# All twelve gate and val chunks by seven products, the stores of narrowed blocks moved to SyncE, small products kept in front of two y columns only

## The chip, the cores and the metric

The kernel runs on one core of a Trainium2 chip. The metric is the time on the device in microseconds (us), the median over several runs. The engines are TensorE (PE; its weight loads are shown as PEld), VectorE (DVE), ScalarE (ACT), GpSimd (POOL) and SyncE (SP), which here only issues transfers.

## What is computed

The reference is an attention layer followed by two feed-forward layers, on 896 tokens (2 batches of 448) with 12 heads of 64:

```python
attn = softmax(mask(q @ k.T / 8)); x = (attn @ v)           # 896 x 768
h = x @ w_in                                                # 768 -> 2048
g = where(h >= 1, h, where(h <= -1, 0, (h + 1) ** 2 / 4))
y = g @ w_out                                               # 2048 -> 768
out = (silu(y @ w_gate) * (y @ w_val)) @ w_out2             # 768 -> 1536 -> 768
```

The weights reach the kernel as 64 bit floats, and the kernel itself makes 32 bit floats of them.

## The kernel before

**Number form.** A value is held as a high part and a low part, both in the reduced form fp32r: ScalarE casts the high part, VectorE subtracts it from the value for the low part (`split`). A product of two such values is three matmuls: high by high, high by low, low by high. All matmuls of the later stages have 128 x 128 weights and 448 columns.

**Stages.** The tokens are two groups g of 448 columns. First come attention and, mixed into it, the first half of h = x w_in (in 16 chunks f of 128 rows). Then follow the rest of h, and y = g w_out in 6 columns d of 128 rows, each cut in three (`OUT_CUTS`) with both groups in turn. Then come gate and val, in 12 chunks f, and last the product with w_out2 (the last stage), in seven products k with three pairs p each.

**Eight and seven products.** A chunk of gate and val is a product of a 2 x 2 block matrix (gate and val by the two halves of y's rows) with a 2 x 2 block matrix (halves by groups). `eight(f, ws)` does it directly: 8 block products of 9 matmuls. `seven(f, ws)` uses Strassen's scheme in Winograd's form: 7 block products of 9 matmuls, for which sums of weight blocks and of blocks of y are needed. T1 to T4 are the sums of y; they are collected in `sums12` and `sums34` while y is made (L735 to L739), finished with the last column (L756 to L758) and split into the tiles `th` and `tl` (T[0] to T[3]). `SEVEN` lists the chunks by seven: 1 to 10. Chunks 0 and 11 go by eight. In `seven`, products 1 and 2 use gate weights and Y of group 0, product 3 sums of weights and T[1], product 4 T[0], product 5 T[2], product 6 Y of group 1 (second half) and product 7 T[3]. Products 1, 3, 5 and 7 add up in the same PSUM tile, which ScalarE copies out to `one`, `two` and `three` after products 1, 3 and 5. The sums of weights (`Weights.sums`) are `ws`, with the parts `sh`, `sl`, `vh`, `vl`.

**Weights.** The class `Weights` prepares the weights in the order of their use: load (SP), narrow from 64 to 32 bits (`narrow`, three VectorE operations, L110, L113, L116), cast and subtract (L221, L222). Four buffers hold the parts; `room` says whether the next may be started, and `tick` issues a step of this work after a product. So the order written in the program follows the products; a scheduler then sets the order on each engine.

**Narrowed aside.** `narrow_apart` narrows the chunks in `APART` (3, 4, 6, 8, 9) and the blocks W21 of w_out2 during y, in 26 half blocks of 128 x 384 (`araw` into `at`), and stores them in HBM, from where they come back as 32 bit floats. SP loads the raw blocks into two buffers, ACT issues the stores. `S_TICKS` is the number of its steps issued after each third of a column and group (one more in the first third).

**Small products.** `strip` is a matmul of one weight column and eight columns of data whose result nobody reads. It stands in front of chunks 1 and 2 of h (`STRIPS`), of y columns 0 and 3 (`Y_STRIPS`, for both groups), of gate and val chunks 1 and 5 (`V_STRIPS`) and of the first product of the last stage.

**Last stage.** `u_terms` makes the terms of u for the seven products, each from u of chunks 0 to 5 (Z11, Z12) or 6 to 11 (Z21, Z22). W11 and W12 are narrowed into tiles of the pool `quads`; W21 and W22 come from HBM.

Of the kernel before, what the change touches and what calls it, by code (L numbers as in the profile page):

```python
# [8 lines left out]
F32 = mybir.dt.float32  # L9
# [14 lines left out]
N = 448  # L24
# [4 lines left out]
WB = 768  # L29
# [17 lines left out]
SEVEN = (1, 2, 3, 4, 5, 6, 7, 8, 9, 10)  # L47
TICK8 = (1, 2)
PIN0, PIN1 = 2, 28
APART = (3, 4, 6, 8, 9)  # L50
# [4 lines left out]
S_TICKS = 2  # L55
S_LOW = "V"
PINNED = 2
STRIPS = (1, 2)
Y_STRIPS = (0, 3)
V_STRIPS = (1, 5)  # L60
# [13 lines left out]
def fused_kernel(ctx: ExitStack, tc: tile.TileContext, qk, v, w_in, w_out, w_gv, w_o2, out):  # L74
# [47 lines left out]
    def narrow_apart(pool):  # L122

        parts = [(narrowed, f, w_gv[f], k) for f in APART for k in range(0, 2 * WB, PART)]
        parts += [(stored, ("W21", p), w_o2[p, 1, 0], k) for p in range(OUT_PAIRS) for k in range(0, WB, PART)]
# [11 lines left out]
        for p, (home, f, src, k) in enumerate(parts):  # L137
# [9 lines left out]
            if p:  # L147
                nc.scalar.dma_start(out=outs[p - 1][0], in_=outs[p - 1][1])
        nc.scalar.dma_start(out=outs[-1][0], in_=outs[-1][1])

    class Weights:
# [24 lines left out]
        def room(self, i):  # L176

            if I_GV <= i < I_O2 and (i - I_GV) % 2 and (i - I_GV) // 2 in SEVEN and not sums_pool:
                return False
            return i < EARLY or self.used > i - (EARLY if i < EARLY + WBUFS else WBUFS)  # L180
# [9 lines left out]
        def operations(self):  # L190
            for at, (kind, i, src, n) in enumerate(self.seq):
                self.load(at + 1)
                f, val = divmod(i - I_GV, 2)
                if kind == "apart":
# [3 lines left out]
                    nc.scalar.dma_start(out=stored["W22", i], in_=t.bitcast(F32))  # L198
# [13 lines left out]
                if f in SEVEN and i < I_O2:  # L212
# [16 lines left out]
        def term(self, at, i):  # L229
# [3 lines left out]
            if k < 2:  # L233
# [26 lines left out]
        def sums(self, i, gate, val):  # L260
# [7 lines left out]
            sh = sums_pool[0].tile([128, 3 * HALF], F32R, tag="sh", name="sh")  # L268
            sl = sums_pool[0].tile([128, 3 * HALF], F32R, tag="sl", name="sl")
# [42 lines left out]
    for i, (src, n) in enumerate(srcs):  # L312
# [3 lines left out]
        if i >= I_O2:  # L316
            k, p = divmod(i - I_O2, OUT_PAIRS)
            src = w_o2[p, 0, k] if k < 2 else None
# [386 lines left out]
    side.close()  # L705
    yctx = ExitStack()
# [40 lines left out]
    sums_pool.append(mctx.enter_context(tc.tile_pool(name="sums_p", bufs=2, reuse_waits="tile")))  # L747
    tctx = ExitStack()
    tp = tctx.enter_context(tc.tile_pool(name="tp", bufs=1, side="right", reuse_waits="tile"))
    Y = {(g, c): [yp.tile([128, N], F32R, name=f"y{part}{g}_{c}") for part in "hl"] for c in range(KC) for g in range(2)}  # L750
    for g in range(2):
        for c in range(KC - 1):
            split(raw[g][:, c], *Y[g, c])
        split(pss[g][:, :N], *Y[g, KC - 1])
# [31 lines left out]
    def eight(f, ws):  # L786
        for g in range(2):
            pss = [bank() for _ in range(2)]
            for s in range(2):
                for half in range(2):  # L790
                    add(pss[s], ws[s], half * HALF, chunks(g, half), not half, bool(half))
                    W.tick(TICK8[half])
                if g:
                    W.free(I_GV + 2 * f + s)
# [177 lines left out]
```

## Time and profile before

| | us |
|---|---|
| median of 3 runs | 584.44 |
| lowest and highest | 584.02, 584.60 |
| the profiled execution | 584.13 |
| its span, first to last instruction | 582.3 |
| PE busy | 572.1 |
| DVE busy | 492.2 |
| ACT busy | 287.8 |
| y: 225.4 to 342.4 | 117.0 |
| gate and val: 342.4 to 501.3 | 158.9 |
| w_out2: 501.3 to the end | 81.0 |

All times in the trace count from the span's start. The durations of matmuls overlap, since they are pipelined: the cost of one is the step from its start to the start of the next. "Idle before" counts only where the engine had something to wait for. Times of y, gate and val and w_out2 are read off the first matmuls of the stages.

### The profile page before, as it was taken

How to read it: one execution, taken by the hardware profiler on the slowest of the kernel's cores; microseconds unless marked ns; L12 is line 12 of the kernel's file. 1: busy time of each engine (PE TensorE's matmuls, PEld its weight loads, DVE VectorE, ACT ScalarE, POOL GpSimd, SP SyncE). 2: the span in 40 equal slices, each digit the busy share in tenths (PEclk: the TensorE clock that was granted, in tenths of full speed). 3: DMA queues.
4: the chain of work that ended last, by engine and by line, in shares of the span. 5: the costliest groups of instructions: out<-in, count | busy, mean ns of one | idle time of the engine just before them, and what ended most of it. 6: DMA issues, size and time to landing. Idle time of an engine off the chain costs nothing.

```text
span 582.3 us, 8615 instructions
## 1 busy us (share of the span) xinstructions
PE 572.1 (98%) x3177; PEld 498.9 (86%) x3181; DVE 492.2 (85%) x937; ACT 287.8 (49%) x580; POOL 1.2 (0%) x8
## 2 busy tenths in 40 slices
PE   9999999999999999999999999999999999999997
PEld 4766777778999999999999999999999999999996
DVE  3999999995977888886878979999896498999980
ACT  3999999983434443211120374544454344356431
POOL 0000000000000000000000000000000000000000
PEclk9999999999999999999999999999999999999999
DMA  8565641331331235787778702354542143710011
GB/s 261 180 182 181 200 129 66 93 126 54 106 112 39 77 105 164 222 270 249 221 259 261 243 35 60 130 163 115 184 136 66 59 135 97 314 66 17 16 64 63
DMA packets 26009, 80.38 MB, mean 138 GB/s; under 512 B 2928, under 2 KB 10672, under 8 KB 25968
## 3 DMA queue, kind: packets, MB, share of 16 engines
q1 hardware_dynamic: 21792, 73.54, 39.7%
q10 hardware_dynamic: 4176, 6.29, 2.9%
q8 instruction: 25, 0.41, 0.3%
q14 instruction: 16, 0.13, 0.1%
HBM read 70.78 MB, written 9.04 MB: 137 GB/s over the span
## 4 chain that ended last, share of the span: by engine, by line
PE 87%; ACT 6%; DVE 5%; issue 1%; DMA 0%; ACTq 0%
PE mm L92 36%; PE mm L776 27%; PE mm L911 13%; ACT p L496 3%; PE mm L94 2%; PE mm L579 1%; PE s L92 1%; PE o L92 1%; PE t L94 1%; PE s L94 1%; PE o L94 1%; DVE s L474 1%; ACT p L512 1%; ACT pt L532 1%; PE t L92 1%
## 5 line engine op out<-in xcount | busy, mean ns | idle before, releaser
L221 ACT CAST wh<-wt 128x768 fp32r<-128x768 f32 (+1 forms) x43 | 34.8, 813 | 88.9 <-PE mm L92 60.0
L92 PE MATMUL mm<-gh,wh 128*128 128x448 f32 x192 | 70.5, 367 | 0.0
L92 PE MATMUL mm<-gl,wh 128*128 128x448 f32 x192 | 70.1, 365 | 0.0
L92 PE MATMUL mm<-gh,wl 128*128 128x448 f32 x192 | 70.1, 365 | 0.0
L92 PE MATMUL mm<-xh,wh 128*128 128x448 f32 x165 | 63.0, 382 | 1.2 <-DVE q L368 1.2
L496 ACT ACTIVATE p<-s,mx 112x112 f32<-112x112 f32 (+3 forms) x96 | 47.1, 509 | 11.6 <-DVE mx L482 9.3
L92 PE MATMUL mm<-xl,wh 128*128 128x448 f32 x138 | 50.7, 368 | 0.0
L92 PE MATMUL mm<-xh,wl 128*128 128x448 f32 x138 | 50.7, 368 | 0.0
L222 DVE TENSOR_TENSOR wl<-wt,wh 128x768 fp32r<-128x768 f32 (+1 forms) x43 | 39.4, 916 | 11.7 <-ACT wh L221 11.1
L113 DVE SCALAR_TENSOR_TENSOR wt<-wraw,wt 128x768 int32<-128x768 int32 (+1 forms) x51 | 47.0, 921 | 0.8
L116 DVE SCALAR_TENSOR_TENSOR wt<-wraw,wt 128x768 int32<-128x768 int32 (+1 forms) x51 | 46.9, 920 | 0.5
L911 PE MATMUL mm<-uh,oh 128*128 128x448 f32 x126 | 46.4, 368 | 0.0
L911 PE MATMUL mm<-ul,oh 128*128 128x448 f32 x126 | 46.2, 367 | 0.0
L911 PE MATMUL mm<-uh,ol 128*128 128x448 f32 x126 | 46.0, 365 | 0.0
L776 PE MATMUL mm<-yh,wh 128*128 128x448 f32 x108 | 39.8, 369 | 0.0
L776 PE MATMUL mm<-yl,wh 128*128 128x448 f32 x108 | 39.6, 367 | 0.0
L776 PE MATMUL mm<-yh,wl 128*128 128x448 f32 x108 | 39.6, 367 | 0.0
L92 PEld LDWEIGHTS mm<-gh,wh 128*128 128x128 f32 x192 | 36.1, 188 | 3.2
L92 PEld LDWEIGHTS mm<-gh,wl 128*128 128x128 f32 x192 | 36.1, 188 | 2.9
L92 PEld LDWEIGHTS mm<-gl,wh 128*128 128x128 f32 x192 | 36.1, 188 | 2.8
L92 PEld LDWEIGHTS mm<-xh,wh 128*128 128x128 f32 x165 | 31.0, 188 | 7.0 <-issue 2.1
L776 PE MATMUL mm<-th,sh 128*128 128x448 f32 x90 | 33.1, 368 | 0.0
(164 smaller groups left out, 1389.8 us busy)
## 6 DMA issues: line engine op xcount, KB each, us to landing
wraw<-w_in SPq DMA_DIRECT2D x16, 768.0 KB, 4.3
wraw<-w_gv SPq DMA_DIRECT2D x14, 768.0 KB, 4.5
wraw<-w_out SPq DMA_DIRECT2D x12, 768.0 KB, 4.8
araw<-w_gv SPq DMA_DIRECT2D x20, 384.0 KB, 4.9
wraw<-w_o SPq DMA_DIRECT2D x9, 768.0 KB, 4.4
n<-at ACTq DMA_DIRECT2D x26, 192.0 KB, 4.5
qk_t<-qk SPq DMA_DIRECT2D x12, 336.0 KB, 3.3
wraw<-n SPq DMA_DIRECT2D x5, 768.0 KB, 4.2
```

The source lines that it names most:

```text
L92: return product(*args, **kw)
L94: return tc.keep_in_program_order(product(*args, **kw))
L113: yield nc.vector.scalar_tensor_tensor(out=t, in0=w[:, :, 1], scalar=-0x40000000, in1=t, op0=ALU.bitwise_and, op1=ALU.bitwise_or,)
L116: yield nc.vector.scalar_tensor_tensor(out=t, in0=w[:, :, 0], scalar=29, in1=t, op0=ALU.logical_shift_right, op1=ALU.bitwise_or,)
L221: nc.scalar.copy(out=wh[:, :n], in_=t)
L222: (nc.vector if i < LOW_V else nc.gpsimd).tensor_tensor(out=wl[:, :n], in0=t, in1=wh[:, :n].bitcast(F32), op=ALU.subtract,)
L474: nc.vector.tensor_tensor_reduce(out=part, in0=part, in1=mask[:, S - w:], scale=-0.125, scalar=3.0e38, op0=ALU.add, op1=ALU.min, accum_out ...
L496: nc.scalar.activation(out=p[:, h, off:off + w], in_=s[:C, h, off:off + w], func=AF.Exp, bias=mx[:, i, h:h + 1], scale=-1.0 if j in TTR el ...
L512: nc.scalar.mul(out=ph, in_=ph, mul=r)
L532: (nc.vector.tensor_copy if turns[k % len(turns)] == "V" else nc.scalar.copy)(out=pts[u][:, :, off:off + w], in_=st[k].pop("t")[:C, :, :w])
L776: nc.tensor.matmul(out=ps[:, :N], lhsT=w[a][:, sl], rhs=rows[c][b], start=(first and c == i == 0), stop=(last and c == i == 2), skip_group ...
L911: nc.tensor.matmul(out=ps, lhsT=w[a][:, sl], rhs=rows[c][b], start=(not more and c == e == 0), stop=(c == 5 and e == 2), skip_group_check= ...
```

## The change

`SEVEN` and `eight` go away: all twelve chunks go by seven products. The buffers of the sums are split into two pools, one for even chunks (`sums_a`, opened ahead of y) and one for odd chunks (`sums_b`, opened behind y); `room` lets the sums of a val be made as soon as their pool is open. Y tiles of group 1, first half, which only `eight` read, are no longer made: 9 pairs of Y tiles are left of 12. The pools for the last stage, `ua` and `qa`, are opened ahead of the T tiles and not after chunk 10.

The blocks W12 are narrowed aside as well: six more half blocks, 32 in all, with `S_TICKS` at 3. They come back into buffers of the sums when the last stage begins. `APART` is now 2, 4, 6, 8, 9.

The stores of narrowed blocks, those of W22 among them, are issued by SP and no longer by ACT. All small products but those of y are dropped. The order of PSUM banks is set once more ahead of the last stage.

```diff
--- before.py
+++ after.py
@@ -44,20 +44,17 @@
 TURN1 = "A"
-SEVEN = (1, 2, 3, 4, 5, 6, 7, 8, 9, 10)
-TICK8 = (1, 2)
 PIN0, PIN1 = 2, 28
-APART = (3, 4, 6, 8, 9)
+APART = (2, 4, 6, 8, 9)
 PART, PART_BUFS = 384, 2
...
 BEFORE = {4: (0,), 6: (1,), 8: (2,)}
-S_TICKS = 2
+S_TICKS = 3
 S_LOW = "V"
 PINNED = 2
-STRIPS = (1, 2)
+STRIPS = ()
 Y_STRIPS = (0, 3)
-V_STRIPS = (1, 5)
 TTR = (2, 3)
@@ -122,7 +119,7 @@
         parts = [(narrowed, f, w_gv[f], k) for f in APART for k in range(0, 2 * WB, PART)]
-        parts += [(stored, ("W21", p), w_o2[p, 1, 0], k) for p in range(OUT_PAIRS) for k in range(0, WB, PART)]
+        parts += [(stored, (w, p), w_o2[p, a, 1 - a], k) for w, a in (("W21", 1), ("W12", 0)) for p in range(OUT_PAIRS) for k in range(0, WB, PART)]
         raws, outs = [], []
@@ -145,8 +142,8 @@
             if p:
-                nc.scalar.dma_start(out=outs[p - 1][0], in_=outs[p - 1][1])
-        nc.scalar.dma_start(out=outs[-1][0], in_=outs[-1][1])
+                nc.sync.dma_start(out=outs[p - 1][0], in_=outs[p - 1][1])
+        nc.sync.dma_start(out=outs[-1][0], in_=outs[-1][1])
@@ -175,7 +172,10 @@
-            if I_GV <= i < I_O2 and (i - I_GV) % 2 and (i - I_GV) // 2 in SEVEN and not sums_pool:
+            f, val = divmod(i - I_GV, 2)
+            if I_GV <= i < I_O2 and val and len(sums_pool) <= f % 2:
+                return False
+            if i >= I_O2 and len(quads) <= ((i - I_O2) // OUT_PAIRS > 1):
                 return False
@@ -195,7 +195,7 @@
                     stored["W22", i] = apart.tile([128, WB], F32, name=f"o{i}")
-                    nc.scalar.dma_start(out=stored["W22", i], in_=t.bitcast(F32))
+                    nc.sync.dma_start(out=stored["W22", i], in_=t.bitcast(F32))
                     continue
@@ -209,7 +209,7 @@
                     t = t.bitcast(F32)
-                if f in SEVEN and i < I_O2:
+                if I_GV <= i < I_O2:
                     if not val:
@@ -230,7 +230,13 @@
             name = TERMS[k][1]
-            if k < 2:
+            if i == I_O2:
+                two = sums_pool[0].tile([128, 2 * WB], F32, tag="s", name="W12", bufs=1)
+                one = sums_pool[0].tile([128, 3 * HALF], F32, tag="sh", name="W12_2")
+                for q, t in enumerate((two[:, :WB], two[:, WB:], one[:, :WB])):
+                    nc.sync.dma_start(out=t, in_=stored["W12", q])
+                    quad["W12", q] = t
+            if k < 1:
                 t = quads[0].tile([128, WB], I32, name=f"{name}_{p}")
@@ -265,8 +271,9 @@
             t = sums_pool[0].tile([128, 4 * HALF], F32, tag="s", name="ws", bufs=1)
-            sh = sums_pool[0].tile([128, 3 * HALF], F32R, tag="sh", name="sh")
-            sl = sums_pool[0].tile([128, 3 * HALF], F32R, tag="sl", name="sl")
+            pool = sums_pool[(i - I_GV) // 2 % 2]
+            sh = pool.tile([128, 3 * HALF], F32R, tag="sh", name="sh")
+            sl = pool.tile([128, 3 * HALF], F32R, tag="sl", name="sl")
             s1, s2, s3, s4 = (t[:, k * HALF:(k + 1) * HALF] for k in range(4))
@@ -315,7 +322,7 @@
             k, p = divmod(i - I_O2, OUT_PAIRS)
-            src = w_o2[p, 0, k] if k < 2 else None
+            src = w_o2[p, 0, 0] if k < 1 else None
         seq.append(("op", i, src, n))
@@ -703,6 +710,7 @@
     side.close()
+    sums_pool.append(ctx.enter_context(tc.tile_pool(name="sums_a", bufs=1, side="right", reuse_waits="tile")))
     yctx = ExitStack()
@@ -744,14 +752,15 @@
     yp = mctx.enter_context(tc.tile_pool(name="yp", bufs=1, reuse_waits="tile"))
-    sums_pool.append(mctx.enter_context(tc.tile_pool(name="sums_p", bufs=2, reuse_waits="tile")))
+    sums_pool.append(mctx.enter_context(tc.tile_pool(name="sums_b", bufs=1, reuse_waits="tile")))
+    places = [ctx.enter_context(tc.tile_pool(name="ua", bufs=1, side="right", reuse_waits="tile"))]
+    quads.append(ctx.enter_context(tc.tile_pool(name="qa", bufs=1, side="right", reuse_waits="tile")))
     tctx = ExitStack()
     tp = tctx.enter_context(tc.tile_pool(name="tp", bufs=1, side="right", reuse_waits="tile"))
-    Y = {(g, c): [yp.tile([128, N], F32R, name=f"y{part}{g}_{c}") for part in "hl"] for c in range(KC) for g in range(2)}
-    for g in range(2):
-        for c in range(KC - 1):
-            split(raw[g][:, c], *Y[g, c])
-        split(pss[g][:, :N], *Y[g, KC - 1])
+    YS = [(0, c) for c in range(KC)] + [(1, c) for c in range(3, KC)]
+    Y = {(g, c): [yp.tile([128, N], F32R, name=f"y{part}{g}_{c}") for part in "hl"] for g, c in YS}
+    for g, c in YS:
+        split(raw[g][:, c] if c < KC - 1 else pss[g][:, :N], *Y[g, c])
     ps = [p[:, :N] for p in pss]
@@ -783,17 +792,6 @@
-    def eight(f, ws):
-        for g in range(2):
-            pss = [bank() for _ in range(2)]
-            for s in range(2):
-                for half in range(2):
-                    add(pss[s], ws[s], half * HALF, chunks(g, half), not half, bool(half))
-                    W.tick(TICK8[half])
-                if g:
-                    W.free(I_GV + 2 * f + s)
-            gated(f, g, *(p[:, :N] for p in pss))
-
     def seven(f, ws):
@@ -801,8 +799,6 @@
-        if f in V_STRIPS:
-            strip(tiles[0], gate[0], chunks(0, 0)[0][0])
         add(a, gate, 0, chunks(0, 0), True, True)
@@ -855,7 +851,6 @@
-    places = []
     u_queue = u_terms()
@@ -864,15 +859,11 @@
         ws = [W.get(I_GV + 2 * f), W.get(I_GV + 2 * f + 1)]
-        if f > SEVEN[-1]:
+        if f == FC2 - 1:
             next(u_queue)
-        (seven if f in SEVEN else eight)(f, ws)
-        if f == SEVEN[-1]:
-            tctx.close()
-            places.append(ctx.enter_context(tc.tile_pool(name="ua", bufs=1, side="right", reuse_waits="tile")))
-            quads.append(ctx.enter_context(tc.tile_pool(name="qa", bufs=1, side="right", reuse_waits="tile")))
-        if f > SEVEN[-1]:
-            next(u_queue)
+        seven(f, ws)
+    next(u_queue)
+    tctx.close()
     mctx.close()
@@ -890,6 +881,7 @@
+    banks.sort(key=lambda pool: pool is mm_a)
     held = {}
@@ -903,8 +895,6 @@
             ps = held[SAME.get(k, k), p][:, :N]
-            if k == p == 0:
-                strip(held[k, p], w[0], rows[0][0])
             for c in range(6):
```

## Rows read from the trace of the kernel before

**Rows 1.** Page, part 1: busy us (share of the span) xinstructions of each engine.
```profile
PE 572.1 (98%) x3177; PEld 498.9 (86%) x3181; DVE 492.2 (85%) x937; ACT 287.8 (49%) x580; POOL 1.2 (0%) x8
```
**Rows 2.** Chain that ended last, in order of time: start, us, what.
```profile
287.75 54.83 PE mm L92 x270
342.57 14.59 PE mm L776 x72
357.17 51.77 PE mm L776 x252
...
501.49 77.49 PE mm L911 x378
```
**Rows 3.** Timeline of PE at starts of chunks: start, us, engine, line, operation, tiles.
```profile
342.41 0.36 PE L776 MATMUL mm<-yh,wh 128*128 128x448 f32 x1
...
357.00 0.17 PE L336 MATMUL mm<-yh,wh 128*1 128x8 f32 x1
...
357.32 0.36 PE L776 MATMUL mm<-yl,wh 128*128 128x448 f32 x1
...
369.96 0.37 PE L776 MATMUL mm<-yh,wh 128*128 128x448 f32 x1
...
382.90 0.37 PE L776 MATMUL mm<-yh,wh 128*128 128x448 f32 x1
...
486.44 0.37 PE L776 MATMUL mm<-yh,wh 128*128 128x448 f32 x1
...
501.32 0.17 PE L336 MATMUL mm<-uh,oh 128*1 128x8 f32 x1
```
**Rows 4.** Busy time by stretch (y, its columns 4 and 5), clock, DMA share, GB/s.
```profile
225.42:342.42 117.00, 117.00 (x580) 108.14 (x581) 94.47 (x166) 24.95 (x41) 0.00 (x0) 1.00 0.74 235
...
303.30:322.90 19.60, 19.60 (x98) 18.17 (x97) 17.17 (x32) 3.25 (x5) 0.00 (x0) 1.00 0.86 279
322.90:342.40 19.50, 19.50 (x98) 18.07 (x97) 16.20 (x28) 8.04 (x15) 0.00 (x0) 1.00 0.46 153
```
**Rows 5.** Timeline of DVE from y into gate and val.
```profile
343.72 0.61 DVE L756 TENSOR_TENSOR traw<-mm,traw 128x448 f32<-128x448 f32 x1
...
345.32 5.95 DVE L104 TENSOR_TENSOR tl<-traw,th 128x1344 fp32r<-128x1344 f32 x4
...
357.75 0.95 DVE L280 TENSOR_TENSOR sl<-ws,sh 128x768 fp32r<-128x768 f32 x1
```
**Rows 6.** Timeline of ACT in the same stretch; in brackets idle before, and its end.
```profile
342.61 0.54 ACT L103 CAST yh<-mm 128x448 fp32r<-128x448 f32 x1 [0.95 <-PE mm L92]
343.04 5.08 ACT L103 CAST th<-traw 128x1344 fp32r<-128x1344 f32 x4
```
**Rows 7.** Groups by line, DVE: count | busy us, mean ns | idle before, its end.
```profile
L280 DVE TENSOR_TENSOR sl<-ws,sh 128x384 fp32r<-128x384 f32 (+1 forms) x20 | 14.8, 749 | 3.1 <-ACT sh L279 3.1
...
L116 DVE SCALAR_TENSOR_TENSOR at<-araw,at 128x384 int32<-128x384 int32 x26 | 14.4, 553 | 0.4
...
L110 DVE TENSOR_SCALAR at<-araw 128x384 int32<-128x384 int32 x26 | 9.2, 355 | 11.9 <-DMA araw<-w_gv 9.8 <-DMA araw<-w_o 2.1
...
L271 DVE TENSOR_TENSOR ws<-wt 128x384 f32<-128x384 f32 x5 | 2.8, 556 | 0.1
```
**Rows 8.** Timeline of DVE in y; last, by tile, landing times of raw blocks.
```profile
229.72 0.35 DVE L110 TENSOR_SCALAR at<-araw 128x384 int32<-128x384 int32 x1
...
308.10 0.35 DVE L110 TENSOR_SCALAR at<-araw 128x384 int32<-128x384 int32 x1
...
320.01 0.68 DVE L222 TENSOR_TENSOR wl<-wt,wh 128x512 fp32r<-128x512 f32 x1
...
324.48 0.36 DVE L110 TENSOR_SCALAR at<-araw 128x384 int32<-128x384 int32 x1
...
DMA to landing us min/median/max: 3.7/4.1/5.3
```
**Rows 9.** Waits of ACT, from 300 us to 345 us: us in total, times, longest.
```profile
ACT wh L221 <- DMA n<-at: 6.5, 1, 6.5
```

## Prediction

> **What bounds the kernel now.** I read the page's busy times first. PE is busy for 572.1 of 582.3 us, and DVE for 492.2 [rows 1]: the reader is to see that PE is the bound as a whole and that DVE isn't far behind. Then the chain that ended last, in order of time. From 287.75 us on it holds PE pieces alone (four of them stand here), each beginning where the one before it ends, with no other engine between them until the last product of the kernel [rows 2]. So in y, in gate and val, and in the last stage each matmul taken away shortens the kernel, and each wait put in front of one lengthens it. Third, PE's timeline at the starts of chunks tells what a chunk costs, and how fast matmuls follow each other: chunk 0 (eight products, 72 matmuls) lasts from 342.41 to 357.00, 14.59 us, or 0.2026 us for each matmul; chunk 2 (seven products, 63 matmuls) from 369.96 to 382.90, 12.94 us, or 0.2054; chunk 11 (eight) from 486.44 to 501.32, 14.88 us, or 0.2067 [rows 3]. The pace between matmuls thus has levels some 2% apart, and they aren't waits.
>
> **Chunks 0 and 11 by seven.** Each goes from 72 matmuls to 63 and should last as long as chunk 2 does. Chunk 0 gains 14.59 - 12.94 = 1.65 us, chunk 11 gains 14.88 - 12.94 = 1.94 us [rows 3]; together **-3.59 us**, all on the path.
>
> **The small products.** Five are dropped that this kernel issues on the path: two in h, two in chunks 1 and 5, one ahead of the last stage (those of y stay). One costs what the step over it takes beyond a usual one: 357.32 - 357.00 = 0.32 against 0.20, 0.12 us [rows 3]; five are -0.6 us. What they gave back is the quicker pace behind them, at most 0.2067 - 0.2026 = 0.0041 us a matmul. For chunks 1 and 5 that holds for 18 matmuls each, since the others of a chunk run at chunk 2's mean anyway: +0.15. In h I take at most three chunks of 18, +0.22. In the last stage the 378 matmuls last 77.49 us, 0.2050 each [rows 2]; at the slow level throughout they would last 0.64 longer, at the quick one 0.9 less. I take +0.3 there. Sum: **+0.1 us**, with bounds of -0.8 and +0.7 for the pace, which I can't tell ahead since buffers move too.
>
> **What is late at the start of chunk 0.** This is the largest unknown. By eight, chunk 0 needed Y alone for 14.6 us, and the splitting of T1 to T4 was hidden behind it. By seven, the third product needs T's second block (made of the last column of y), the val sums, and ScalarE's copy `one` of the first product, since it adds to the same PSUM tile. It is due after 18 matmuls: 342.41 + 18 x 0.2026 = 346.06 us. In the trace ScalarE casts the last Y at 342.61 and then the four T blocks until 343.04 + 5.08 = 348.12 [rows 6]; VectorE makes the three T differences from 343.72 on, at 0.53 us each, and the four low parts from 345.32, at 1.47 us each, so that the second of these is done at about 348.3 [rows 5]. If this order stays, the copy `one` (0.54, as the 342.61 cast of the same size) stands behind the four casts in ScalarE's queue: 348.12 + 0.54 = 348.66, and PE waits for 2.6 us. The low parts alone would hold it for 348.3 - 346.27 = 2.0 us, as the second matmul reads them. That is the upper end. The lower end has the first T block split earlier (its data are complete after the third column of y) and `one` copied ahead of the last two casts: then the second block's cast starts at 344.3 and ends at 345.6, its low part needs 1.5 more, 347.2, and the wait is 347.2 - 346.27 = 0.9 us. Three Y splits fewer (about 0.61 on VectorE for each, as the difference of the same size in [rows 5]) free room for the early one. The trace does not show the new order; it shows the four casts together behind the Y cast, which is nearer to the upper end, so I take **+2.0 us**. Nothing hides it, and nothing later gives it back, because PE has no other waits to absorb.
>
> **Val sums, chunk 0 and 1.** Chunk 0's sums are made during the last column of y, where their buffers now exist. They cost VectorE four sums of 0.556, two low parts with a mean of 0.749 and two as short as a sum [rows 7], 4.8 us, instead of one whole low part of 0.95 (as the one at 357.75 in [rows 5]): +3.9 us there. For chunk 1 the first sums were ready at 357.75 + 0.95 = 358.70 [rows 5], 2 us before their use, 18 matmuls behind the small product (357.12 + 18 x 0.2026 = 360.77, [rows 3]). Now VectorE has five evictions of chunk 0 instead of two (three more, some 0.6 each) in front of them, and their use comes 1.65 us earlier, but 2.0 later by the wait above: 358.70 + 1.8 = 360.5 against 360.77 - 1.65 + 2.0 = 361.1. I take no second wait; if the first wait is short this one costs up to 1.4 us, so the two are one term with the range 0.9 to 2.7.
>
> **More narrowing beside y.** W12's six half blocks join 26 others: 6 x (0.355 + 0.553 + 0.553) = 8.8 us on VectorE (the second step of the three is as long as the third) [rows 7]. VectorE is busy for 94.5 of the 117.0 us of y [rows 4]; with 8.8 and 3.9 more and 1.9 less (three Y splits) it comes to 105.3, so 11.7 are left, about what it spent waiting for raw blocks in the whole run (11.9, [rows 7]). The steps per column go from 14 to 20, so that all 96 operations are issued in 4.8 columns, 6.7 blocks in 19.5 us: 2.9 us for a block. In the trace, five blocks that start from 308.10 to 324.48 took 3.28 us each, most of their starts waiting for the load, whose landing took 3.7 to 5.3 us [rows 8]. So blocks will be late: the 32nd starts between 229.7 + 31 x 2.9 = 320 and 229.7 + 31 x 3.28 = 331 us. The weights of y are ready far ahead, which covers that: the last ones at 320.01 + 0.68 = 320.7 [rows 8], used 24 matmuls before y's end, from 337.5 on; the last column has 16.2 us of VectorE work in 19.5 now, 4 blocks (5.9) among it [rows 4], so 16.2 - 5.9 + 3.9 - 1.9 = 12.3 us must follow in the 11 us behind a block at 331. I cost it at nothing, with an upper end of +3.5 us (below). That chunk 2 is narrowed aside in place of chunk 3 moves VectorE work from 357 to 383 us to some 13 us later, which relieves the fuller stretch: zero. In return W12's three narrowings (up to 2 x 1.46 = 2.9 us each by the same rows) leave the last stage, where VectorE was close behind PE; worth nothing, as PE didn't wait there.
>
> **Stores by SyncE.** The ScalarE queue loses 26 stores in y and three of W22 behind it, and with them waits such as the 6.5 us that a weight cast stood behind one [rows 9]; those waits were hidden by weights made ahead, so zero. On SyncE each store waits for the last operation of its own block, which was over before; the raw block and weight loads queued behind it wait no longer for it than for their buffers. SP's issue of 32 stores is small. By the Trainium skill (DMA: Bandwidth & Descriptors, Queues, rings and completion order) SP and ACT each have a row of rings on the same 16 engines, an engine takes turns between rows and takes one row's descriptors in order; by that rule a load now stands behind a store, where it ran beside it. No row here shows stores and loads on one queue; the rival below gives it a price from rows.
>
> **Chunk 11 and the last stage.** Chunk 11's val now needs sums, +3.9 us of VectorE, against W12's narrowing less; the W12 loads wait for chunk 11's sums to be read, and have the first three products of the last stage (54 x 0.205 = 11 us) to land. Zero, upper end +1.
>
> **The sum**, against the profiled execution (584.13 us, of which 582.3 is the span): 584.13 - 3.59 + 0.1 + 2.0 = 582.6. The median of the runs is 0.31 higher, so **582.9 us**.
>
> **Rivals.**
> (a) The start of chunk 0 is hidden: T's blocks and `one` come in an order that leaves at most 0.9 us. 580.9 to 581.8. For it: ScalarE is idle for most of y, and the first T block's data are early. Against it: its trace order in [rows 6].
> (b) The gain is eaten: the casts stay in front of `one` and chunk 1's sums are late as well, a wait of 2.7 to 4 us. 583.6 to 584.9. For it: VectorE is full from 342 to 360 us already.
> (c) **Slower**: the narrowing beside y falls behind, and VectorE reaches the T differences late. It decides from the block pace: at 3.15 us a block the last one starts at 327.4 and 12.3 us of work end with y; at 3.5 it starts at 338.2, and T and the sums are 8 to 10 us late. A store of 0.2 MB at the 279 GB/s of [rows 4] takes 0.7 us; if each load waits for that, half of it falls on each block: 3.28 + 0.35 = 3.6. That is where the queue rule just named would lead. At a middle pace of 3.28 to 3.4 the end is 1.5 to 5 us late: 584.4 to 588, I say 586. Against it: at 3.28 there were stores in flight as well, and VectorE's own waits fill up when it has more to do.
>
> **How the numbers follow.** Forecast (a wait of 0.9 to 2.7 us, 581.8 to 583.6): 0.44. (a) 0.17, (b) 0.19, (c) 0.20. A measurement of this kernel can tell about 0.2%, 1.17 us, from no change, so faster means under 583.27. That takes (a) and some 0.37 of the forecast: 0.54. Same: the rest of the forecast, and most of (b): 0.25. Slower (over 585.6): (c) and the end of (b): 0.21. The range runs from 580.8 (no wait) to 586.5, which takes in half of (c).
>
> **What would show it.** Chunks 0 and 11 at about 12.9 us of matmuls each; a gap in PE about 3.7 us after chunk 0 begins, ended by `one` or by a low part of T; no other gap. In y the raw-block waits of VectorE grow and the last block starts at about 325 to 331 us. The prediction is wrong if that gap isn't there, if PE waits in y or at the first matmul of chunk 0, or if the pace of h or the last stage shifts by more than 0.002 us a matmul.

## The result, and the profile after

The changed kernel takes **589.26 us** (588.9 to 589.94) against 584.42 us: 0.85% slower, ratio 1.0085 with a 95% interval of [1.0068, 1.0103]. I had predicted 582.9, within 580.8 to 586.5.

The profiled run took 589.94 us, 588.1 of it span. First part 1 of the page of after, which answers to [rows 1].

```profile
PE 572.2 (97%) x3154; PEld 496.9 (84%) x3158; DVE 503.4 (86%) x963; ACT 292.6 (50%) x591; POOL 1.2 (0%) x8
```

PE has 23 instructions fewer and is busy just as long, in a longer span. So its matmuls got slower somewhere, and it waits somewhere. The chain that ended last (start, us, what) says where; before, this stretch held PE alone [rows 2].

```profile
342.41 0.55 DVE at L113
...
348.03 3.29 DVE yl L101 x6
...
353.26 0.53 DVE traw L765
...
354.85 1.48 DVE tl L101
...
356.37 150.54 PE mm L785 x733
506.91 77.66 PE mm L901 x378
```

From 342 to 356 us VectorE sets the end: the last operation on a narrowed block, then (left out here) the low parts of chunk 0's sums and the narrowing of chunk 1's weights, the low parts of Y, the T differences, the first low part of T. The differences begin at 353.26 here, 9.5 us later than before [rows 5]; behind 356.37 PE runs through to the last stage. PE's timeline at the end of y, and the busy time of y and of the next 14 us (busy us of PE, PEld, DVE, ACT, POOL, granted clock, DMA share, GB/s):

```profile
342.28 0.37 PE L89 MATMUL mm<-gh,wl 128*128 128x448 f32 x1
344.38 0.47 PE L785 MATMUL mm<-yh,wh 128*128 128x448 f32 x1 [1.74 <-ACT yh L100]
347.30 0.74 PE L785 MATMUL mm<-yl,wh 128*128 128x448 f32 x1 [2.44 <-DVE yl L101]
347.83 0.57 PE L785 MATMUL mm<-yh,wl 128*128 128x448 f32 x1
...
352.23 0.57 PE L785 MATMUL mm<-yl,wh 128*128 128x448 f32 x1
...
355.19 0.47 PE L785 MATMUL mm<-th,sh 128*128 128x448 f32 x1 [1.31 <-ACT th L100]
```

```profile
225.40:342.30 116.90, 116.90 (x581) 108.07 (x579) 96.02 (x172) 19.11 (x29) 0.00 (x0) 1.00 0.81 251
342.30:356.40 14.10, 8.53 (x26) 6.05 (x24) 14.06 (x24) 10.53 (x18) 0.00 (x0) 0.76 0.20 70
```

PE waits 1.74 + 2.44 + 1.31 = 5.5 us. Besides, after the first two waits with a single matmul between them, the granted clock falls: its mean is 0.76 in the stretch, and from 347.83 to 352.23 most of twelve matmuls (some left out here) follow each other at 0.373 us, the lower level of 1.2 GHz, where it was 0.203 to 0.207 [rows 3]. From 347.30 to 353.51 seventeen matmuls take 6.21 us instead of 3.5: 2.7 us more, most of it by the clock.

Why VectorE is late shows in its waits in y (us in total, times, longest), its first and last operation on a block, and the landing of raw blocks, last line:

```profile
DVE at L107 <- DMA araw<-w_gv: 11.8, 10, 2.2
DVE at L107 <- DMA araw<-w_o: 6.6, 5, 2.2
```

```profile
227.60 0.35 DVE L107 TENSOR_SCALAR at<-araw 128x384 int32<-128x384 int32 x1
...
340.73 0.36 DVE L107 TENSOR_SCALAR at<-araw 128x384 int32<-128x384 int32 x1 [0.55 <-DMA araw<-w_o]
...
DMA to landing us min/median/max: 3.7/4.9/7.0
```

VectorE was busy for 94.5 us of y before [rows 4] and is for 96.0 now. With 9 us more to do in y it did 1.5 more there; its waits for raw blocks went from 11.9 [rows 7] to 18.4 us. The 32nd block starts at 340.73, (340.73 - 227.60) / 31 = **3.65 us a block**, 1.6 us before y ends, and all that VectorE must do for chunk 0 stands behind it.

### The profile page after: what moved, and what is told of

Same layout as the page of the kernel before. It is cut to its first block, busy times and chain, and to the rows that moved or that the text cites. A ratio compares the mean times of both kernels' runs of the same rounds, so it can differ in the third digit from the quotient of the medians.

```text
span 588.1 us, 8613 instructions
## 1 busy us (share of the span) xinstructions
PE 572.2 (97%) x3154; PEld 496.9 (84%) x3158; DVE 503.4 (86%) x963; ACT 292.6 (50%) x591; POOL 1.2 (0%) x8
## 4 chain that ended last, share of the span: by engine, by line
PE 64%; DVE 14%; DMA 13%; ACT 6%; issue 2%; DVEq 0%; ACTq 0%
PE mm L785 26%; PE mm L89 15%; PE mm L901 13%; DMA araw<-w_gv 8%; DMA araw<-w_o 4%; ACT p L503 3%; PE mm L91 2%; DVE at L110 2%; PE mm L586 1%; DVE wt L113 1%; DVE at L107 1%; PE s L89 1%; DVE wt L110 1%; PE o L89 1%; PE t L91 1%
## 5 line engine op out<-in xcount | busy, mean ns | idle before, releaser
L221 ACT CAST wh<-wt 128x768 fp32r<-128x768 f32 (+1 forms) x41 | 33.1, 812 | 85.6 <-PE mm L89 62.5
L785 PE MATMUL mm<-th,sh 128*128 128x448 f32 x108 | 39.8, 368 | 1.3 <-ACT th L100 1.3
L785 PE MATMUL mm<-tl,sh 128*128 128x448 f32 x108 | 39.7, 367 | 0.1
L785 PE MATMUL mm<-th,sl 128*128 128x448 f32 x108 | 39.3, 364 | 0.0
L222 DVE TENSOR_TENSOR wl<-wt,wh 128x768 fp32r<-128x768 f32 (+1 forms) x41 | 37.5, 914 | 0.6
L259 ACT CAST oh<-W 128x768 fp32r<-128x768 f32 x21 | 17.6, 836 | 27.5 <-PE mm L901 13.3
```

The costliest lines, as they stand in the source:

```text
L221: nc.scalar.copy(out=wh[:, :n], in_=t)
L222: (nc.vector if i < LOW_V else nc.gpsimd).tensor_tensor(out=wl[:, :n], in0=t, in1=wh[:, :n].bitcast(F32), op=ALU.subtract,)
L259: nc.scalar.copy(out=wh, in_=quad[name, p])
L785: nc.tensor.matmul(out=ps[:, :N], lhsT=w[a][:, sl], rhs=rows[c][b], start=(first and c == i == 0), stop=(last and c == i == 2), skip_group ...
```

## The experiments

The letters in the expectations name theories of that one batch; the text says them in words. All times stand against runs of the kernel before on the same chip. In the table, "steps" are the narrowing steps issued for a column of y, "raw" the raw buffers, "T" is the start of the T differences, which follow the last column of y. The times of blocks and of T are those of the profiled runs.

| kernel | blocks | steps | raw | us a block | last block | T | time | ratio |
|---|---|---|---|---|---|---|---|---|
| before | 26 | 14 | 2 | 3.95 | 328.4 | 343.7 | 584.4 | 1 |
| after | 32 | 20 | 2 | 3.65 | 340.7 | 353.2 | 589.3 | 1.0085 |
| e_act_stores | 32 | 20 | 2 | 3.66 | 341.2 | 353.5 | 592.9 | 1.0145 |
| e_b_sp | 26 | 14 | 2 | 3.99 | 330.0 | 344.3 | 584.5 | 0.9998 |
| e_raw3 | 32 | 20 | 3 | 3.54 | 337.6 | 349.9 | 587.7 | 1.0053 |
| e_fill | 32 | 20 | 2 | 3.60 | 339.7 | 352.2 | 592.6 | 1.0145 |
| e_w12_late | 26 | 14 | 2 | 4.18 | 331.7 | 343.3 | 582.4 | 0.9967 |
| e_steps | 26 | 20 | 2 | 3.62 | 317.8 | 343.5 | 582.7 | 0.9968 |
| e_work | 26 + 6 again | 20 | 2 | | | 343.4 | 582.9 | 0.9972 |
| e_drop9 | 28 | 20 | 2 | 3.60 | 325.6 | 345.1 | 581.6 | 0.995 |
| e_small | 48 of 256 | 32 | 3 | 2.40 | 340.3 | 350.1 | 588.1 | 1.0057 |
| e_small2 | 48 of 256 | 32 | 2 | 3.35 | 385.3 | 354.7 | 616.3 | 1.0549 |
| e_small_drop9 | 42 of 256 | 32 | 3 | 2.37 | 324.7 | 343.6 | 580.6 | 0.9937 |
| e_strips | 42 of 256 | 32 | 3 | 2.38 | 325.4 | 344.3 | 581.1 | 0.995 |

**Is it the queue of the stores?** The changed kernel with the stores back on ScalarE (the edit of one of the two lines stands here), and the kernel before with its stores on SyncE:

```diff
-                nc.sync.dma_start(out=outs[p - 1][0], in_=outs[p - 1][1])
+                nc.scalar.dma_start(out=outs[p - 1][0], in_=outs[p - 1][1])
```

> The changed kernel with one part undone: the stores of the half blocks narrowed beside y are issued by ACT again, as before; all else stays. In the changed kernel VectorE waited 18.4 us for raw blocks in y, their landing took 4.9 us (median; 4.3 before), and the 32nd block began at 340.7 us. Theory A (one queue slows the loads): landing goes back to about 4.3 us, the waits to about 12, the last block begins near 333, and the time is 584 to 586 us. Theory B (two raw buffers and 32 blocks make the pace, the queue is nothing): landing and waits stay, 588.5 to 589.5 us.

> The kernel before, with its 26 half-block stores issued by SyncE instead of ScalarE; nothing else changes. If the queue of the stores makes blocks late (a load standing behind a store), the landing of a raw block rises from a median of 4.3 us to about 4.9 and VectorE's waits for raw blocks from 11.8 us to 15 or more; the time stays within 0.5 us of the kernel before all the same, because by eight products chunk 0 leaves 14 us for what is late: 584.0 to 584.9. If the queue is nothing, landing stays at 4.3 us, waits near 11.8 us, and the time at 584.4.

e_act_stores measured 592.86 us, ratio 1.0145 [1.0129, 1.016]. The block pace is the same, and so is the landing:

```profile
341.22 0.36 DVE L107 TENSOR_SCALAR at<-araw 128x384 int32<-128x384 int32 x1 [0.93 <-DMA araw<-w_o]
...
DMA to landing us min/median/max: 3.8/4.8/7.0
```

e_b_sp measured 584.46, ratio 0.9998 [0.9988, 1.0007], with a median landing of 4.7 us against 4.3. So with the stores on one queue with the loads, the median landing is at most 0.4 us longer, and the kernel before takes no longer; the queue isn't the cause of the late T. But e_act_stores, above both of its ranges, takes 3.6 us more than after: in the changed kernel the stores on SyncE gain time. Its profiled run takes 1.9 us more than after's, and 1.6 of that lies behind T's first low part, where from 356.40 to 362.00 its granted clock is 0.70 and after's 1.00. What sets the clock apart there, and the rest of the 3.6 us, no run shows.

**A third raw buffer.** Three raw buffers, two loads ahead, and one of the three narrowed buffers given up for the space:

```diff
-PART, PART_BUFS = 384, 2
+PART, PART_BUFS = 384, 3
         load()
+        load()
...
-            t = pool.tile([128, PART], I32, tag="t", name="at", bufs=3)
+            t = pool.tile([128, PART], I32, tag="t", name="at", bufs=2)
```

> The changed kernel with three raw buffers in place of two for the half blocks (and two narrowed ones in place of three, for room), and loads issued two blocks ahead. Theory B (the cycle load, landing, three operations over two buffers sets the pace): the 18.4 us of waits fall under 6, the last block begins before 328 us, the T differences come within 2 us of y's end, and the time is 582 to 584 us. Rival C (VectorE has too much work in y whatever it waits for): waits fall but VectorE is busy instead, T differences still 5 us or more behind y's end, 586 us or more.

It measured 587.69 us (584.82 to 589.31), ratio 1.0053 [1.0034, 1.0072]. The waits of VectorE in y (us, times, longest) show why so little was won:

```profile
DVE at L107 <- DMA n<-at: 17.3, 18, 2.2
```

The waits for raw blocks are gone, and nearly as many us are spent waiting for a narrowed buffer to be stored. Another wait took the place of the one removed. So the theory of the two raw buffers missed with its last block (before 328; it came at 337.6) and its time (582 to 584); the time of its rival came, but not its cause, since VectorE is busy for 96.4 us of y, hardly more than after's 96.0. Three of both at this size weren't tried.

**Is it the clock?** 24 matmuls whose result isn't used, ahead of chunk 0's first product, so that PE works while it would wait:

> The changed kernel with 24 idle matmuls of 448 columns in front of the first product of chunk 0 (their result is overwritten by a later product), so that PE is busy while it waits for Y there. In the changed kernel 15 matmuls of chunk 0 ran at steps of 0.37 us, at half the clock, behind the wait. Theory D (VectorE's lateness sets the start of the sums products, the slow matmuls lie beside it): the clock stays up, but PE then waits for T until about 355 us all the same; 588.5 to 590 us. Rival E (the slow clock costs 15 x 0.17 = 2.5 us and more of its own): 585 to 587 us.

It measured 592.64 us, ratio 1.0145 [1.013, 1.016]. The wait of PE, and two windows:

```profile
PE mm L786 <- ACT one L807: 4.6, 1, 4.6
```

```profile
342.30:351.00 8.70, 8.70 (x45) 8.05 (x43) 8.67 (x15) 6.76 (x13) 0.00 (x0) 1.00 0.31 113
356.40:362.00 5.60, 4.97 (x14) 4.47 (x15) 5.57 (x7) 2.83 (x5) 0.00 (x0) 0.54 0.00 0
```

Both theories missed the time. The clock stays full where after's first waits were, and falls after the next long wait: `one` now stands behind all four T casts on ScalarE (at 356.46 us, though the first product ends near 350; in after it stood behind the first cast, at 351.00), PE waits 4.6 us for it, and its next matmuls run at 0.373 us. So the fill changed ScalarE's order too, and what the clock alone costs in after isn't measured by it. In these runs the low clock came behind such waits, here of 4.6 us and in after of 1.74 and 2.44 us with one matmul between; not behind every one: after the 1.31 us at 355.19 in after it stays at 1.00.

**Six blocks fewer, slower steps.** W12 is narrowed in the last stage again (three narrowings into the same buffers); chunks 0 and 11 by seven, SyncE's stores and the small products stay as changed:

```diff
-S_TICKS = 3
+S_TICKS = 2
-        ... for w, a in (("W21", 1), ("W12", 0)) ...
+        ... for w, a in (("W21", 1),) ...
```

> The changed kernel without W12 among the blocks narrowed beside y: 26 half blocks at the old rate of steps; W12 is loaded raw and narrowed in the last stage, into the same buffers of the sums. Chunks 0 and 11 by seven, stores by SyncE stay. Theory F (the six blocks more and the faster steps make VectorE late): T differences within 2 us of y's end, a wait of 1 to 3 us in chunk 0, 582 to 584 us. Rival G (chunk 0's sums in the last column of y, or the queue of the stores, make it late): still 5 us late, 586 us or more.

It measured **582.41 us**, ratio 0.9967 [0.9958, 0.9977], below the kernel before. T's differences come at 343.26, and in chunk 0 PE waits for nothing:

```profile
342.30:356.40 14.10, 14.10 (x71) 12.72 (x70) 13.35 (x18) 11.38 (x15) 0.00 (x0) 1.00 0.12 33
```

What is left shows in the last stage: its first matmul, PE's wait there, and the chain from there on:

```profile
496.96 0.37 PE L903 MATMUL mm<-uh,oh 128*128 128x448 f32 x1
...
517.35 0.47 PE L903 MATMUL mm<-uh,oh 128*128 128x448 f32 x1 [1.05 <-ACT oh L261]
```

```profile
577.24 0.53 ACT osb L919
```

577.24 - 496.96 = 80.28 us. In after, read in the same way, it is 584.59 - 506.74 = 77.85: with chunk 11 by seven, narrowing W12 in the last stage costs 2.4 us, of which 1.4 are recorded as waits of PE. So the late VectorE at chunk 0 comes from the six blocks or from the faster steps, and three kernels tell these apart.

**Steps, work or transfers?** e_steps is e_w12_late with `S_TICKS = 3`. e_work is e_steps with the last six blocks narrowed twice: VectorE's work of 32 blocks with the transfers of 26.

```diff
-            for i, op in enumerate(narrow(raws[p], t)):
+            again = 2 if p >= len(parts) - 6 else 1
+            for i, op in enumerate(op for _ in range(again) for op in narrow(raws[p], t)):
```

> The kernel of e_w12_late (26 blocks beside y, W12 narrowed in the last stage; 582.41 us) with 20 steps of narrowing for each column of y again instead of 14, as the changed kernel has. Theory S (the faster steps put narrowing ahead of the weights, sums and splits on VectorE): T's differences, at 343.26 us in e_w12_late, come several us later and the time is 584 to 588. Theory W (the work of six more blocks) and theory C (32 blocks at 3.65 us each, the load's cycle) both say: last block earlier than 331.7 us, T's differences at 343 to 344, 582.0 to 582.8.

> The kernel of e_steps, in which the last six of the 26 blocks are narrowed twice on VectorE (18 operations, 8.8 us more, the same result), with no more loads and no more stores than 26. It has VectorE's work of the changed kernel and its steps, but not its transfers. Theory W (VectorE's work makes it late): T's differences near 352 us as in the changed kernel, PE waits at the start of chunk 0 and falls to half clock: 588 to 592, 2.7 us of it in the last stage as in e_w12_late. Theory C (the cycle of loading through two buffers makes it late, and the extra work fills waits): the last block starts some 4 us later than in e_steps and ends before 338 us, T's differences at 343 to 346, 582.3 to 585.

e_steps measured 582.74 us, ratio 0.9968 [0.9956, 0.998], with T at 343.5: the faster steps don't make T late. First and last block:

```profile
227.33 0.35 DVE L107 TENSOR_SCALAR at<-araw 128x384 int32<-128x384 int32 x1
...
317.84 0.36 DVE L107 TENSOR_SCALAR at<-araw 128x384 int32<-128x384 int32 x1 [0.43 <-DMA araw<-w_o]
```

26 blocks at the faster steps run at (317.84 - 227.33) / 25 = 3.62 us, as 32 do (3.65): at 20 steps a column the pace is the same, whatever the number of blocks. e_work measured 582.86 us, ratio 0.9972 [0.9961, 0.9984]. y and T in e_work:

```profile
225.40:342.30 116.90, 116.90 (x580) 108.07 (x580) 104.38 (x189) 24.73 (x42) 0.00 (x0) 1.00 0.73 228
```

```profile
343.37 0.61 DVE L768 TENSOR_TENSOR traw<-mm,traw 128x448 f32<-128x448 f32 x1
```

VectorE is busy for 104.4 us of y, close to the 105.3 that I had added up, and is on time; its waits for raw blocks fall from 14.8 us in e_steps to 10.7. So work alone doesn't make it late. What does is what six more blocks bring besides their work: six more rounds of load, narrowing and store through the same buffers.

**Fewer rounds.** The changed kernel without chunk 9 in `APART`, 28 blocks, W12 kept beside y:

> The changed kernel with chunk 9's four blocks taken out of the narrowing beside y (28 blocks instead of 32); chunk 9 is narrowed from raw weights in its place among gate and val, and W12 stays beside y, so the last stage needs not wait for it. If block number times block pace sets the lateness (27 x 3.65 us behind the first start at 227.6: last block at 326), T's differences come at 343 to 345, no wait in chunk 0 above 0.5 us, and the time is 579.8 to 581.2 (584.4 less 4.1 for chunks 0 and 11), below e_w12_late by its last-stage wait. If narrowing chunk 9 in place makes VectorE late there, PE waits at chunk 9 or 10 and the time is 581.5 to 583. If lateness has another cause than the blocks, T's differences stay near 350 us: 586 to 589.

It measured 581.58 us (580.43 to 583.3), ratio 0.995 [0.9934, 0.9965], with 3.60 us a block. T comes at 345.09, at the upper end of what I gave, and the time is 0.4 us over my range. It lies in the range of the rival, by which PE waits at chunk 9 or 10; but the profile has no such wait. In the profiled run PE was 0.8 us late when y began, and chunk 0 begins at 343.5 instead of 342.5; why isn't known.

**Other rounds.** The same bytes in blocks of 256 columns, with three raw buffers and two loads ahead (e_small, shown here) or two raw buffers and one load ahead (e_small2), 32 steps a column:

```diff
-PART, PART_BUFS = 384, 2
+PART, PART_BUFS = 256, 3
-S_TICKS = 3
+S_TICKS = 5
         load()
+        load()
```

> The changed kernel with the same bytes narrowed beside y, cut into 48 blocks of 256 columns instead of 32 of 384, with three raw buffers instead of two (two loads ahead), three for the narrowed blocks as before and 32 steps for a column. Theory C1 (time per block is landing plus narrowing shared among the raw buffers): (4 + 1.0 + 0.5) / 3 = 1.85 us a block, or VectorE's own pace; the last block starts before 328, T's differences come at 343 to 346 as in e_work, and the time is 579.8 to 582. Theory C2 (the transfers of 32 blocks fill what the DMA engines give, 251 GB/s, however they are cut): the last block near 340 us, T's differences near 350, 586 to 590.

> As e_small, with two raw buffers. Theory C1: the landing hardly gets shorter with the block, so (4 + 1.0 + 0.5) / 2 = 2.75 us a block and 48 blocks take some 130 us: the last starts behind the end of y, near 350 us or later, T's differences come 10 us or more later than in the changed kernel, and the time is 596 to 612. Theory C2 (transfers fill the engines): as the changed kernel, T's differences near 353, 588 to 590.

e_small2 measured 616.28 us, ratio 1.0549 [1.0533, 1.0564], above even the range of the theory that landing, shared among the buffers, sets the pace (596 to 612), and far above the other's, by which the transfers fill the DMA engines (588 to 590). Its last block and its landing:

```profile
385.28 0.29 DVE L107 TENSOR_SCALAR at<-araw 128x256 int32<-128x256 int32 x1 [3.42 <-DMA araw<-w_o]
...
DMA to landing us min/median/max: 2.8/4.3/6.4
```

A block of two thirds the bytes lands in 4.3 us instead of 4.9, so more and smaller rounds through two buffers take longer. Over y it moves 208 GB/s at a DMA share of 0.68, where after has 251 at 0.81: as a mean over y, the engines weren't full. T comes at 354.7, less late than I had given, since here it stands ahead of the last blocks in VectorE's order; the sums and weights of the next chunks stand behind them, and PE waits for those. e_small measured 588.06 us (585.43 to 589.29), ratio 1.0057 [1.0038, 1.0076]. Here the theory of landing missed with its last block (before 328), T and time, and all figures of the other came: last block at 340.3, T at 350.05, 588.06 us. VectorE's group and its only wait for a block:

```profile
L110 DVE SCALAR_TENSOR_TENSOR at<-araw,at 128x256 int32<-128x256 int32 x48 | 20.3, 423 | 1.0
L113 DVE SCALAR_TENSOR_TENSOR at<-araw,at 128x256 int32<-128x256 int32 x48 | 20.3, 422 | 1.0
L107 DVE TENSOR_SCALAR at<-araw 128x256 int32<-128x256 int32 x48 | 13.9, 289 | 8.1 <-DMA n<-at 7.6
```

No wait for raw blocks is left, but the narrowing now costs 20.3 + 20.3 + 13.9 = 54.5 us instead of 32 x 1.46 = 47, and it waits 7.6 us for the stores. 7.5 + 7.6 us take up the 18.4 that the landing gave back, except for 3: T comes at 350.05, 3.1 us earlier than in after. The busy time of y in e_small:

```profile
225.40:342.30 116.90, 116.90 (x579) 108.08 (x579) 103.84 (x226) 23.37 (x39) 0.00 (x0) 1.00 0.79 251
```

It moves as much as after, at a DMA share of 0.79, so as a mean the engines aren't full here either. But landing and full engines can't be told apart as causes by these runs: in the 15 waits of VectorE for raw blocks in after, 18.4 us in all, the DMA share averages 0.96 and the rate 321 GB/s. A block that VectorE waits for lands while the engines are full, with it and with other transfers; at other times they have room. And since 32 blocks' worth of bytes comes late with three raw buffers too (e_raw3, e_small), the two raw buffers aren't the whole of it.

**Both together.** e_small without chunk 9 in `APART`, 42 blocks:

> As e_small, with chunk 9 narrowed in its place among gate and val, so 42 small blocks beside y. Theory C1: like e_small, T's differences at 343 to 344, no wait of PE above 0.5 us in chunk 0, and with y not started late 579.6 to 581. Theory C2: 28/32 of the bytes, like e_drop9, 581 to 582.

It measured **580.64 us** (580.28 to 581.33), ratio 0.9937 [0.9922, 0.9952], the lowest median of all (the intervals of e_drop9 and e_strips overlap with it). That is in the range of the theory of landing and 0.4 us below the other's. Its chain is PE alone again, and PE at the point where I had expected a wait, with ScalarE's row for `one`, reads:

```profile
342.46 155.05 PE mm L786 x756
497.51 77.66 PE mm L902 x378
```

```profile
345.94 0.66 PE L786 MATMUL mm<-th,sh 128*128 128x448 f32 x2
346.44 0.37 PE L786 MATMUL mm<-yh,wh 128*128 128x448 f32 x1
...
347.06 0.36 PE L786 MATMUL mm<-tl,sh 128*128 128x448 f32 x1
```

```profile
342.93 1.32 ACT L100 CAST th<-traw 128x1344 fp32r<-128x1344 f32 x1
344.32 0.53 ACT L804 COPY one<-mm 128x448 f32<-128x448 f32 x1
344.75 3.75 ACT L100 CAST th<-traw 128x1344 fp32r<-128x1344 f32 x3
```

**The small products.** e_small_drop9 with the five dropped small products put back:

> The kernel of e_small_drop9 (580.64 us) with the five dropped small products put back where the kernel before has them: two in h, one in chunk 1 and in chunk 5, one ahead of the last stage. By the term of the prediction (dropping costs 0.1 us, with bounds from a gain of 0.8 to a loss of 0.7) this gives 580.5, within 579.9 to 581.4: h at the quicker 0.203 us a matmul up to about 155 us again, for 0.1 us of PE at each small product. If the small products still buy a quicker pace behind each chunk that has one, chunks 1 and 5 and the last stage shorten by some 0.5 us or more each and the time is below 579.8; if they buy nothing here, 581.0 to 581.3.

It measured 581.05 us, ratio 0.995 [0.9936, 0.9964]. The intervals of the two overlap; the difference of 0.4 us isn't resolved. Its last stage takes 77.49 us, as before, against 77.66.

## Why the prediction was wrong

**What bounds the kernel**: right. PE does, and each wait put in front of it lengthens the kernel.

**Chunks 0 and 11 by seven, -3.59**: right. Where VectorE is on time, gate and val take 155.05 us (e_small_drop9) instead of 501.49 - 342.57 = 158.92 [rows 2]: -3.87, the small products of chunks 1 and 5 among it.

**The small products, +0.1**: within its bounds. e_strips doesn't resolve it.

**Start of chunk 0, +2.0**: wrong as a term. With VectorE on time it is zero; in e_small_drop9 no step of PE there is over 0.3 us. Two things that the trace of before couldn't show made it so. The lower-end order came: the first T block was cast first and `one` stands ahead of the other three casts. And PE's own order changed as well: three matmuls on Y were put between the first matmuls on th and the first on tl, so tl is read at 347.06, not 346.27, and the first of the low parts is done by then. So rival (a)'s place and order were right for a kernel that is on time. In after, too, `one` stood ahead of three casts (at 351.00); there, the differences themselves were late.

**Narrowing beside y, costed at nothing: the step that failed.** Its sum of VectorE's work, 105.3 us, was right (104.4 in e_work), and so was the conclusion that the work fits. What failed is the pace of a block, and under it the sentence that VectorE's own waits fill up when it has more to do. For work alone they do (e_work). More blocks bring their own waits, since a wait for landing is part of each block's round: a raw buffer is loaded, narrowed and given back, and two buffers share that. One round in after, from a load through the first and the last operation on the block to the next load into the same buffer:

```profile
240.86 0.33 SPq L130 DMA_DIRECT2D araw<-w_gv  x1
...
245.82 0.36 DVE L107 TENSOR_SCALAR at<-araw 128x384 int32<-128x384 int32 x1 [1.34 <-DMA araw<-w_gv]
...
247.56 0.56 DVE L113 SCALAR_TENSOR_TENSOR at<-araw,at 128x384 int32<-128x384 int32 x1
...
248.14 0.33 SPq L130 DMA_DIRECT2D araw<-w_gv  x1
```

This one takes 7.3 us. The mean round in after takes 7.4: 5.3 from the issue of the load to the first operation (median landing 4.9), 2.0 until the third operation has ended, and the next load 0.03 later. Half of that is the pace. The landing and the three operations alone (0.355 + 0.553 + 0.553 = 1.46 us, [rows 7]) give (4.9 + 1.46) / 2 = 3.2 us, only a floor; the rest is VectorE's other work ahead of and between them. Measured are 3.60 to 3.66 us in every kernel with two buffers, blocks of 384 and 20 steps, with 26, 28 or 32 blocks. I took a pace between 2.9 (the issue of steps) and 3.28 (five blocks of [rows 8]), so the last block at 320 to 331; it came at 340.7. The rows were there: landing 4.1 with a maximum of 5.3 [rows 8] gives (4.1 + 1.46) / 2 = 2.8 to 3.4 without any other work in the round. And even behind a block at 331 the prediction's own 12.3 us of work didn't fit into the 11 us left. With 14 steps a column the three steps of a block are issued every 19.5 x 3 / 14 = 4.18 us, which is the pace of e_w12_late (before has 3.95), so there the steps set it; e_steps, with 20, comes down to 3.62.

**Rival (c)** was the right mechanism with its threshold (3.15 us a block) and, at 3.5, its delay ("T and the sums are 8 to 10 us late"; 9.5 measured). Two things about it were off. Its cause wasn't the stores' queue. By the Trainium skill (DMA: Bandwidth & Descriptors, Queues, rings and completion order) each DMA engine takes the descriptors of one queue in order. The runs put what that can cost here at no more than 0.4 us of landing (4.7 against 4.3 in the kernel before, 4.9 against 4.8 in the changed one) and, in the kernel before, no time. And I priced it at a middle pace, 586, without the clock. From 342.46 to 506.91 after takes 164.45 us, 9.4 more than e_small_drop9: 5.5 of waits, 2.7 of matmuls at the lower clock, and the remaining 1.2 around the waits and restarts, which I only inferred.

**Stores by SyncE, zero**: right for the kernel before (e_b_sp); in the changed kernel they gain 3.6 us (e_act_stores), which the prediction didn't have and no run explains. **Val sums, +3.9 hidden**: right in size; they weren't hidden in after, where they stand behind the last block (sums and their low parts from 341.0 to 345.2), and were in e_work. **Chunk 11 and the last stage, zero**: right (77.66 against 77.49). But I called the three narrowings that leave it worth nothing, because PE didn't wait there. With chunk 11 by seven it does, and loses 2.4 us (e_w12_late). W12 beside y spares that; chunk 9 beside y was one too many.

**What would show it**: I had named a wait of PE at the first matmul of chunk 0 as a sign of error, and that is where it began.

## What to carry to other kernels

An engine that waits for transfers may have slack for more work, but not for more transfers, if each wait belongs to one round through few buffers: take the time of a round (landing, plus use, plus what stands between), divide it by the buffers, and multiply by the rounds. Read the whole round off a trace: landing and the operations alone gave 0.5 to 0.6 us a block too little here (3.2 against 3.65 in after, 2.7 against 3.35 in e_small2), and another buffer may only move the wait (e_raw3). Then ask what stands behind the last round on the in-order engine. A wait of a few us that PE never had before cost half as much again here, as its clock fell. And of two works that compete for one stretch, moving back the one with slack elsewhere (chunk 9) gave 581.6 us, where undoing the whole change gives 584.4.

## What the runs showed of the hardware

- Median landing in these kernels, beside the other transfers of y: 4.3 us (two raw buffers) to 4.7 (three) for blocks of 128 x 256, and 3.9 (three, e_raw3) to 4.9 (two, after) for 128 x 384 of 64 bits. Two thirds of the bytes don't land in two thirds of the time.
- In after's 15 waits for raw blocks in y the DMA share averages 0.96 and the rate 321 GB/s, against 0.81 and 251 over y.
- Two waits of 1.74 and 2.44 us with one matmul between them were followed by about 5 us at the lower level of the granted clock (steps of 0.373 us instead of 0.203 to 0.207). In e_fill, a wait of 4.6 us was followed by some 4 us of the same. A wait of 1.31 us in after (at 355.19) and one of 1.05 in e_w12_late (at 517.35) were followed by none.
- A narrowing operation on 256 columns takes 0.289 and 0.423 us, on 384 columns 0.357 and 0.556: a third of the columns less saves only a fifth to a quarter of the time.
